# A planner's rank table set anew, and fewer unread products ahead of the first attention score

## The chip, the core and the metric

One core of one Trainium2 chip runs the whole program. The metric is the device time of one launch in microseconds. Five engines work side by side, each through its own list of instructions in order: TensorE (PE in the profile, its weight loads PEld), VectorE (DVE), ScalarE (ACT), GpSimd (POOL) and SyncE (SP), which here issues all DMA transfers.

## The reference

Three layers follow each other on a batch of 4, with 576 tokens and 512 features.

```python
# attention: 8 heads of 64; the first four see a window of 32 keys,
# the other four 32 keys with a dilation of 4
scores = scale * q @ k^T, masked; attn = softmax(scores); x = attn @ v
# first feed-forward layer, with token shift (x_prev is x one token back)
xk = mu_k * x + (1 - mu_k) * x_prev;  xr = mu_r * x + (1 - mu_r) * x_prev
k = relu(xk @ w_k);  v = k * k @ w_v;  r = sigmoid(xr @ w_r);  x = r * v
# second feed-forward layer, with a spatial gate
h = relu(x @ w_in);  u, v = h[..., :512], h[..., 512:]
v = (v - mean(v)) / sqrt(var(v) + 1e-6)
out = (u * (w_spatial @ v + b_spatial)) @ w_out
```

The weights come as 64-bit numbers. The kernel turns them into a high and a low part, and nearly every product of it is a sum of three matmuls (high by high, high by low, low by high).

## The kernel before

The program is written as a list of operations. Each call of `add` records one: what it costs in the planner's estimate on each engine that may do it, the function that emits it, what it reads and writes, and a due time `at`. No operation is emitted when it is recorded. At the end `plan.order()` calls `schedule`, which simulates the engines with these estimates: whenever an engine is free, it takes, of the operations that are ready, the one with the lowest rank. The program is then emitted in the order of the planned starts, and each engine runs its own instructions in that order. So the ranks settle the order on every engine and on SP's list of transfers, and for an operation that two engines may do, which of them does it.

The rank comes from `tuned` and the table `TUNE`. Every operation belongs to a group: a tag such as `('soft', 0, 1)` (softmax, batch 0, second half of the heads) and a kind such as `'mx'`, named after the key it writes. A group has four numbers:

```python
more, grow, dve_, pool_ = TUNE.get(g[0], {}).get(g[1], (0, 0, 792, 22))
prio.append(o[5] + more + grow * (k / count[g]))
self.pens.append({"dve": dve_, "pool": pool_})
```

`o[5]` is the due time, `k` the place of the operation within its group. The last two numbers are handicaps in ns that are added to the end that the planner expects on DVE and on POOL when an operation has a choice of engines.

The due times run from -5000 (first loads) over 1000 for each half of a batch in the first feed-forward layer, 10000 to 11200 for the second layer's first part and 12000 to 13500 for its end. The tags that the prediction uses: `start` and `nat` (first loads, masks, constants), `vw` (values of the attention), `qk` (queries and keys turned), `soft` and `val` (softmax and its product with v), `w` and `w2` (weights loaded and turned into two parts), `k`, `r`, `v` with batch and half (the three products of the first feed-forward layer), `x2`, `u2`, `v2`, `vn`, `ws`, `wsb` (second layer up to the normalised v and the spatial weights), `V`, `vx`, `sp`, `out` (spatial product, gate and last product; the batches come in the order 2, 3, 0, 1).

`order` adds one more thing: where the plan leaves PE idle for more than 60 ns during its first 100 us, it fills the gap with unread products, bf16 matmuls of a constant with itself (224 columns) whose result nobody reads. `end` is the end of PE's last operation; it starts at 500, so the first gap begins there. From `end + 30` on a product is put in every 190 ns in stretches that the plan calls cold, and every 96 ns otherwise, until the next planned operation starts.

In the trace the unread products are the matmuls `psT<-const-bfloat16-1.0`. Nearly every instruction has line L464, since one helper records them all, so the tile names have to be read.

Of the kernel before, what the change touches and what calls it, by code (L numbers as in the profile page):

```python
# [36 lines left out]
def blocks(dil):  # L37
# [38 lines left out]
    ('nat', 0): {'nat': (-2902, -363, 792, 22)},  # L76
    ('nat', 1): {'nat': (5726, -4074, 792, 22)},
    ('out', 0): {'ot': (-3920, 26946, 0, -800), 'out': (-31358, -60293, 1500, -300), 'psB': (135303, 18279, 400, 800)},
    ('out', 1): {'ot': (-60907, 27163, 200, 0), 'out': (52992, 57563, -200, 2000), 'psB': (207273, 5538, 200, -800)},
    ('out', 2): {'ot': (101554, 16247, 200, 22), 'out': (100902, 51712, 200, 800), 'psB': (105659, 29563, 200, -300)},  # L80
    ('out', 3): {'ot': (-109427, -3385, 0, 2000), 'out': (103632, 65781, -600, 800), 'psB': (-41413, -9814, -600, 22)},
# [106 lines left out]
class Plan:  # L188
# [208 lines left out]
    def order(self):  # L397
# [4 lines left out]
        for start, i, e in self.out:  # L402
            if e == "pe":
# [12 lines left out]
                end = self.end[i]  # L416
# [2000 lines left out]
```

## Time and profile before

| what | value |
|---|---|
| three runs, median | 578.58 us |
| three runs, lowest and highest | 575.9 and 580.57 us |
| profiled execution, its own time | 577.68 us |
| span in its profile | 575.9 us |
| mean granted TensorE clock | 0.997 |
| PE busy in the span | 555.1 us |
| DVE, ACT, POOL busy | 435.9, 324.2, 178.2 us |

The span runs from the first to the last instruction of the profiled execution; 1.8 us of its time lie around it. An engine's busy time counts its instructions of arithmetic, the unread products among them, and not the waits.

### The profile page before, as it was taken

How to read it: one execution, taken by the hardware profiler on the slowest of the kernel's cores; microseconds unless marked ns; L12 is line 12 of the kernel's file. 1: busy time of each engine (PE TensorE's matmuls, PEld its weight loads, DVE VectorE, ACT ScalarE, POOL GpSimd, SP SyncE). 2: the span in 40 equal slices, each digit the busy share in tenths (PEclk: the TensorE clock that was granted, in tenths of full speed). 3: DMA queues.
4: the chain of work that ended last, by engine and by line, in shares of the span. 5: the costliest groups of instructions: out<-in, count | busy, mean ns of one | idle time of the engine just before them, and what ended most of it. 6: DMA issues, size and time to landing. Idle time of an engine off the chain costs nothing.

```text
span 575.9 us, 14173 instructions
## 1 busy us (share of the span) xinstructions
PE 555.1 (96%) x5715; PEld 517.2 (90%) x5715; DVE 435.9 (76%) x896; ACT 324.2 (56%) x772; POOL 178.2 (31%) x189
## 2 busy tenths in 40 slices
PE   9788999999999999999999999999989999899996
PEld 8676798789999989999999999999989998689985
DVE  6697999888575898782578955598887789975860
ACT  3578987697372775761657654346553654342331
POOL 1022310544773252210100501036971566422000
PEclk9899999999999999999999999999999999999999
DMA  9879662625944364220023210021010240311012
GB/s 250 224 187 190 180 201 39 103 54 115 130 66 71 101 174 140 66 83 1 1 94 128 74 41 1 26 60 74 1 74 1 60 162 1 110 67 62 1 73 92
DMA packets 95425, 51.55 MB, mean 90 GB/s; under 512 B 77504, under 2 KB 85696, under 8 KB 94848
## 3 DMA queue, kind: packets, MB, share of 16 engines
q1 hardware_dynamic: 95360, 50.65, 33.9%
q8 instruction: 45, 0.74, 0.6%
q14 instruction: 20, 0.16, 0.1%
HBM read 41.72 MB, written 8.91 MB: 88 GB/s over the span
## 4 chain that ended last, share of the span: by engine, by line
PE 67%; DVE 10%; POOL 9%; ACT 7%; issue 6%; DMA 2%; SPq 0%; POOLq 0%; DVEq 0%; ACTq 0%
PE psM L464 42%; PE psB L464 15%; PE psT L464 8%; DVE R L464 2%; PE psS L464 2%; POOL wt L464 2%; ACT L464 1%; POOL sq_dt.float32r L464 1%; DVE wf L464 1%; POOL wsT L464 1%; ACT pt L464 1%; POOL X L464 1%; DMA num<-kept 1%; POOL ws L464 1%; POOL VS L464 1%
## 5 line engine op out<-in xcount | busy, mean ns | idle before, releaser
L464 PE MATMUL psM<-xh,wk 128*128 128x288 f32 x512 | 118.3, 327 | 0.7 <-DVE x L464 0.7
L464 PE MATMUL psM<-sq_dt.float32r,wv 128*128 128x288 f32 x768 | 111.7, 298 | 0.3 <-ACT x L464 0.3
L464 PEld LDWEIGHTS psM<-sq_dt.float32r,wv 128*128 128x128 f32 x768 | 104.1, 189 | 2.0 <-ACT x L464 0.9
L464 PEld LDWEIGHTS psM<-xh,wk 128*128 128x128 f32 x512 | 87.4, 188 | 8.1 <-DVE x L464 0.9
L464 PE MATMUL psM<-xh,wr 128*128 128x288 f32 x256 | 60.2, 302 | 0.4 <-ACT x L464 0.2
L464 POOL TENSOR_TENSOR xl<-xm,xh 128x288 fp32r<-128x288 f32 x25 | 25.5, 1029 | 112.7 <-PE psM L464 35.4
L464 PE MATMUL psM<-xl,wk 128*128 128x288 f32 x192 | 56.4, 294 | 0.0
L464 ACT ACTIVATE kr<-psM 128x288 f32<-128x288 f32 x60 | 24.5, 408 | 39.6 <-PE psM L464 38.0
L464 PE MATMUL psB<-wv,X 128*128 128x256 f32 x336 | 43.7, 284 | 1.8 <-DVE num L464 1.5
L464 PEld LDWEIGHTS psM<-xh,wr 128*128 128x128 f32 x256 | 43.6, 188 | 2.0 <-ACT kr L464 0.7
L464 PEld LDWEIGHTS psB<-wv,X 128*128 128x128 f32 x336 | 41.2, 190 | 2.4 <-issue 1.9
L464 PE MATMUL psM<-X,wu 128*128 128x256 f32 x336 | 42.0, 280 | 0.1
L464 PEld LDWEIGHTS psM<-X,wu 128*128 128x128 f32 x336 | 40.4, 188 | 0.3 <-DVE x L464 0.3
L464 PE MATMUL psB<-wo,gh 128*128 128x512 f32 x128 | 39.6, 391 | 0.0
L464 DVE SCALAR_TENSOR_TENSOR xm<-xd,mu,x 128x288 f32<-128x288 f32 x56 | 35.3, 643 | 4.7 <-POOL xl L464 4.3
L464 PE MATMUL psM<-xl,wr 128*128 128x288 f32 x128 | 37.8, 295 | 0.5 <-POOL xl L464 0.5
L464 POOL TENSOR_TENSOR sq_dt.float32r<-kr,sq_dt.float32r 128x288 fp32r<-128x288 f32 x29 | 25.9, 902 | 35.0 <-ACT sq_dt.float32r L464 19.1
L464 PEld LDWEIGHTS psM<-xl,wk 128*128 128x128 f32 x192 | 36.2, 189 | 0.0
L464 PE MATMUL psT<-const-bfloat16-1.0 128*128 128x224 bf16 x224 | 28.8, 285 | 2.5 <-issue 1.7
L464 ACT ACT_TABLE_LOAD x23 | 29.5, 1283 | 2.8 <-DVE pr L464 1.7
L464 PEld LDWEIGHTS <-const-bfloat16-1.0 128*128 128x128 bf16 x224 | 23.6, 109 | 5.4 <-issue 2.6
L464 ACT CAST xh<-xm 128x288 fp32r<-128x288 f32 x42 | 18.0, 432 | 17.6 <-PE psM L464 8.8
(265 smaller groups left out, 1245.3 us busy)
## 6 DMA issues: line engine op xcount, KB each, us to landing
vw<-in_v_dram SPq DMA_DIRECT2D x36, 128.0 KB, 3.0
room<-in_moe_w_k_dram SPq DMA_DIRECT2D x8, 512.0 KB, 6.0
room<-in_moe_w_v_dram SPq DMA_DIRECT2D x8, 512.0 KB, 3.8
raw<-in_moe_w_in_dram SPq DMA_DIRECT2D x8, 512.0 KB, 3.7
out_dram<-ot SPq DMA_DIRECT2D x16, 256.0 KB, 2.0
ld<-in_k_dram SPq DMA_DIRECT2D x48, 72.0 KB, 2.7
ld<-in_q_dram SPq DMA_DIRECT2D x48, 72.0 KB, 2.5
vw<-in_v_dram SPq DMA_DIRECT2D x16, 144.0 KB, 4.7
```

The costliest lines, as they stand in the source:

```text
L464: return self.tc.keep_in_program_order(getattr(self.engine, name)(*args, **kw))
```

## The change

All 376 groups, in all 128 tags, get new numbers; no group keeps its four. No operation is added, removed or altered, nor any tile, due time or estimate. The second edit is the number from which the first gap of PE is filled. The core of the diff, with the groups of the tags that the prediction speaks of:

```diff
-    ('qk', 0, 0): {'nT': (3175, 2385, 792, 22)},
-    ('nat', 0): {'nat': (-2902, -363, 792, 22)},
-    ('nat', 1): {'nat': (5726, -4074, 792, 22)},
-    ('vw', 0, 0): {'vw': (1947, -223, 792, 22)},
-    ('vw', 0, 1): {'vw': (5562, 774, 792, 22)},
-    ('w', 'wk', 'ld'): {'raw': (226, 4234, 100, 22)},
-    ('r', 0, 0): {'g': (-10371, -5776, 792, 22), 'psM': (9780, -4754, 792, 22), 'xh': (5314, -10237, 1500, 22), 'xl': (-1491, -1640, 792, -800), 'xm': (2724, 1937, 792, 22)},
-    ('v', 0, 1): {'g': (-810, -767, 792, 22), 'psM': (-2066, 2788, 792, 22)},
-    ('vs', 0, 0): {'vw': (11887, 5366, -600, 300)},
-    ('sp', 3): {'R': (19098, -29678, 0, 300), 'egh': (44866, 6324, -600, 800), 'egl': (-152697, -19248, 0, 800), 'gh': (-9562, 27302, 792, 800), 'gl': (-35280, 17202, -200, 800), 'psB': (-34724, -36529, 792, -800), 'psM': (-30995, 34002, 400, 2000)},
...
+    ('qk', 0, 0): {'nT': (61063, -6021, 0, -300)},
+    ('nat', 0): {'nat': (-35649, 3637, -600, 22)},
+    ('nat', 1): {'nat': (5753, -2082, 1500, 2000)},
+    ('vw', 0, 0): {'vw': (-15144, -10511, 0, 2000)},
+    ('vw', 0, 1): {'vw': (5657, 1020, 200, 0)},
+    ('w', 'wk', 'ld'): {'raw': (339, 3820, -200, -300)},
+    ('r', 0, 0): {'g': (-25879, -841, 792, -800), 'psM': (38606, -2525, -600, 0), 'xh': (106286, 3062, 200, -800), 'xl': (18947, -9071, 792, 300), 'xm': (22826, 2592, 0, -300)},
+    ('v', 0, 1): {'g': (12727, 838, 200, 800), 'psM': (78743, 11012, 400, -800)},
+    ('vs', 0, 0): {'vw': (10892, 17667, 1500, 22)},
+    ('sp', 3): {'R': (33493, -87300, -600, 22), 'egh': (121122, -31373, -600, -800), 'egl': (-136220, -3783, 0, 0), 'gh': (67682, 53762, 1500, 300), 'gl': (-29731, 15, -600, -300), 'psB': (-105640, -34734, -200, 2000), 'psM': (-65533, 36135, 1500, 800)},
...
-        res, end, open_, used = [], 500, set(), False
+        res, end, open_, used = [], 5600, set(), False
```

In the table before, many groups of the first batch have the handicaps 792 and 22 that a group without an entry would get, and their ranks are moved by some twenty thousand at most; in the new one most of these handicaps differ, and ranks are moved by up to a hundred thousand.

## Rows read from the trace of the kernel before

**Rows 1.** The page's busy times by engine (us, share of the span, instructions).

```profile
PE 555.1 (96%) x5715; PEld 517.2 (90%) x5715; DVE 435.9 (76%) x896; ACT 324.2 (56%) x772; POOL 178.2 (31%) x189
```

**Rows 2.** Busy time of each engine by stage (stretch, its length, then each engine).

```profile
11.00:84.00 73.00, 65.18 (x1064) 53.15 (x1063) 62.13 (x123) 54.13 (x164) 15.41 (x14) 0.98 0.80 197
60.00:84.00 24.00, 23.39 (x145) 19.90 (x144) 23.65 (x41) 21.58 (x46) 7.65 (x7) 1.00 0.62 167
84.00:400.00 316.00, 314.28 (x3444) 300.65 (x3443) 235.89 (x489) 190.70 (x450) 90.86 (x103) 1.00 0.32 78
400.00:440.00 40.00, 38.20 (x319) 37.65 (x319) 34.12 (x59) 21.12 (x36) 30.32 (x26) 1.00 0.07 27
460.00:505.00 45.00, 40.82 (x274) 37.83 (x274) 42.60 (x85) 20.41 (x43) 26.25 (x26) 1.00 0.26 91
505.00:566.00 61.00, 61.00 (x352) 54.77 (x351) 40.44 (x108) 21.14 (x51) 7.35 (x8) 1.00 0.15 57
```

**Rows 3.** What PE waited for: total us, times, longest.

```profile
PE psM L464 <- DVE wf L464: 3.3, 2, 2.8
PE psT L464 <- issue: 3.0, 2, 1.7
PE psM L464 <- issue: 2.3, 1, 2.3
PE psS L464 <- issue: 1.6, 1, 1.6
PE psB L464 <- DVE num L464: 1.5, 2, 0.8
```

**Rows 4.** The unread products alone, by stretch (PE, PEld, POOL).

```profile
22.70:31.00 8.30, 7.71 (x59) 6.64 (x59) 0.00 (x0) 0.81 0.81 229
31.00:60.00 29.00, 7.21 (x47) 3.77 (x40) 0.00 (x0) 1.00 0.91 194
60.00:84.00 24.00, 3.62 (x28) 2.52 (x28) 0.00 (x0) 1.00 0.62 167
```

**Rows 5.** Timeline of PE, start to first scores (start, us, what, count).

```profile
0.77 10.09 PE L464 MATMUL psT<-const-bfloat16-1.0 128*128 128x224 bf16 x79 [0.77 <-PEq L2400]
...
11.06 0.93 PE L464 MATMUL psM<-turned,turned 32*32 32x64 f32 x48
```

**Rows 6.** PE alone, before and after the step in its pace.

```profile
0.70:5.30 4.60, 4.53 (x25) 1.00 0.74 246
5.40:10.60 5.20, 5.20 (x56) 1.00 1.28 223
```

**Rows 7.** Timeline of DVE and of SP in the first 26 us.

```profile
4.71 4.50 DVE L464 STREAM_TRANSPOSE turned<-early 128x576 f32<-128x576 f32 x4 [2.78 <-DMA early<-in_k_dram]
...
23.07 1.12 DVE L464 COPY pt<-psT 64x384 f32<-64x384 f32 x2 [0.17 <-PE psT L464]
24.12 0.15 DVE L464 TENSOR_SCALAR st<-st 128x6 f32<-128x6 f32 x1
...
14.65 7.91 SPq L464 DMA_DIRECT2D early<-in_v_dram  x6
22.60 2.68 SPq L464 DMA_DIRECT2D room<-in_moe_w_k_dram  x3
```

**Rows 8.** Instructions begun before two stalls of PE end, and the half-clock stretch.

```profile
0.00:16.53 16.53, 13.48 (x223) 11.66 (x223) 11.23 (x14) 7.18 (x21) 1.54 (x9) 1.00 0.98 268
...
0.00:21.63 21.63, 16.96 (x351) 14.21 (x351) 13.50 (x21) 9.49 (x33) 1.54 (x9) 1.00 0.94 238
...
22.50:25.50 3.00, 3.00 (x18) 2.45 (x17) 2.78 (x8) 1.13 (x8) 0.00 (x0) 0.50 0.75 202
```

**Rows 9.** The page's DMA queue of instruction code (packets, MB).

```profile
q8 instruction: 45, 0.74, 0.6%
```

**Rows 10.** The same gate instruction on DVE, in 460:505 and in 505:566 (mean ns).

```profile
L464 DVE SCALAR_TENSOR_TENSOR R<-x,R 128x288 f32<-128x288 f32 x4 | 4.3, 1098 | 0.0
...
L464 DVE SCALAR_TENSOR_TENSOR R<-x,R 128x288 f32<-128x288 f32 x4 | 1.8, 454 | 0.0
```

More of the change, by code (lines that the diff above doesn't have):

```diff
@@ L56 @@
 TUNE = {
[19 rows of a table removed]
-    ('nat', 0): {'nat': (-2902, -363, 792, 22)},
-    ('nat', 1): {'nat': (5726, -4074, 792, 22)},
[L78 to L81, printed above, removed]
[33 rows of a table removed]
@@ L115 @@
-    ('spill', 0): {'spill': (-124049, 2878, 400, 300)},
-    ('spill', 1): {'spill': (-6568, -5613, 0, 0)},
-    ('start',): {'ident': (5243, -7493, 792, 22), 'identb': (-2035, 973, 792, 22), 'mask': (0, 0, 792, 22), 'mask2': (0, 0, 792, 22), 'pt': (7412, 207, 792, 800), 'xok': (11235, 2251, 792, 22)},
-    ('tail',): {'ed': (-37713, -12930, 200, 300), 'eh': (55031, -1110, -200, 800), 'el': (93554, 2871, 200, 300), 'wt': (85684, -68565, 0, 22)},
-    ('tailu', 0): {'psB': (-76264, 25848, 1500, -300), 'utl': (-166368, 9728, 792, 800)},
@@ L120 @@
-    ('tailu', 1): {'psB': (-146359, 49937, 792, 800), 'utl': (-25714, 9413, -200, 22)},
-    ('tailv', 0): {'psB': (-72892, 31446, 1500, 2000), 'vtl': (-76471, -4488, -200, 2000)},
-    ('tailv', 1): {'psB': (-134513, 18615, -200, 0), 'vtl': (-118272, 5243, -600, -300)},
[16 rows of a table removed]
-    ('val', 0, 0): {'psT': (-5281, 5817, 792, 22), 'x': (-16083, -108, 400, 22)},
-    ('val', 0, 1): {'psT': (-3130, -2324, 792, 22), 'x': (4471, 2599, 0, 22)},
-    ('val', 1, 0): {'psT': (3622, 5837, 792, 22), 'x': (-1516, -3804, 0, 22)},
@@ L142 @@
-    ('val', 1, 1): {'psT': (-7539, -7372, 792, 22), 'x': (-9000, 2119, 1500, 22)},
-    ('val', 2, 0): {'psT': (113980, 6146, 400, 0), 'x': (95825, 15957, 1500, 2000)},
-    ('val', 2, 1): {'psT': (-24445, 36013, 792, 300), 'x': (-128732, -34949, -600, -800)},
-    ('val', 3, 0): {'psT': (3444, -13395, 400, 300), 'x': (92914, -58322, 1500, 300)},
-    ('val', 3, 1): {'psT': (-13877, -8819, 792, 0), 'x': (-27787, 36830, 792, 300)},
[16 rows of a table removed]
-    ('w', 'wiu'): {'low': (70028, -40938, -200, 300), 'num': (55346, -605, -600, 800)},
@@ L164 @@
-    ('w', 'wiu', 'ld'): {'raw2': (-52618, -2354, 0, 0)},
-    ('w', 'wiv'): {'low': (130621, -11407, 792, 300), 'num': (215637, -20046, -600, 300)},
[14 rows of a table removed]
-    ('wvroom',): {'wvroom': (0, 0, 792, 22)},
[4 rows of a table removed]
[19 rows of a table added]
+    ('nat', 0): {'nat': (-35649, 3637, -600, 22)},
+    ('nat', 1): {'nat': (5753, -2082, 1500, 2000)},
+    ('out', 0): {'ot': (25583, 2679, 0, 300), 'out': (-144665, -101352, 1500, 0), 'psB': (110898, 7639, 792, -300)},
+    ('out', 1): {'ot': (333, 22848, 1500, 0), 'out': (46189, 64137, 200, 800), 'psB': (225887, 4579, 1500, 0)},
@@ new lines @@
+    ('out', 2): {'ot': (159270, 16910, 1500, -300), 'out': (64073, 69739, 200, 300), 'psB': (26481, 53919, 0, 2000)},
+    ('out', 3): {'ot': (-136582, -8545, 400, 800), 'out': (163805, 39140, 1500, 2000), 'psB': (37793, -6238, 400, 300)},
[33 rows of a table added]
+    ('spill', 0): {'spill': (-110849, 9986, 1500, 2000)},
+    ('spill', 1): {'spill': (-1206, 33896, 400, 2000)},
+    ('start',): {'ident': (46909, -11681, 792, 22), 'identb': (-42650, -12478, -600, 0), 'mask': (7273, -11647, 1500, -800), 'mask2': (-22564, 13200, 400, 800), 'pt': (1497, -6304, 0, -800), 'xok': (19078, -5180, 0, 300)},
@@ new lines @@
+    ('tail',): {'ed': (-26618, 4131, 792, 300), 'eh': (124111, 20405, 200, 2000), 'el': (129364, 56147, 792, 0), 'wt': (183590, -52436, 400, -800)},
+    ('tailu', 0): {'psB': (-75819, 37467, -600, 2000), 'utl': (-134685, 32141, -600, -800)},
+    ('tailu', 1): {'psB': (-231364, 107397, -600, 22), 'utl': (-87552, -749, -200, 0)},
+    ('tailv', 0): {'psB': (-62599, 49372, 200, 800), 'vtl': (-175319, 32396, -200, 800)},
+    ('tailv', 1): {'psB': (-172671, 29059, -200, -300), 'vtl': (-79316, 28163, 400, -800)},
[16 rows of a table added]
@@ new lines @@
+    ('val', 0, 0): {'psT': (76881, 12666, 1500, 300), 'x': (-93718, -12119, 200, 2000)},
+    ('val', 0, 1): {'psT': (24530, 3459, 200, 22), 'x': (21869, 14497, 400, -300)},
+    ('val', 1, 0): {'psT': (3161, 6992, 200, 800), 'x': (22631, -11997, -600, -800)},
+    ('val', 1, 1): {'psT': (-12793, 21083, -200, -800), 'x': (-10891, -7775, 1500, 0)},
+    ('val', 2, 0): {'psT': (163121, 12068, 0, -300), 'x': (122850, 1744, -200, 0)},
+    ('val', 2, 1): {'psT': (-39083, 58929, 400, 800), 'x': (-59515, -45784, -600, -800)},
@@ L185 @@
+    ('val', 3, 0): {'psT': (-57327, -20764, -200, 800), 'x': (101510, -60419, -200, -300)},
+    ('val', 3, 1): {'psT': (19735, -6516, -200, 22), 'x': (16343, 37837, 1500, 800)},
[16 rows of a table added]
+    ('w', 'wiu'): {'low': (-28276, -51119, 792, -800), 'num': (197080, -22641, -600, 300)},
+    ('w', 'wiu', 'ld'): {'raw2': (102589, -31738, 792, 2000)},
+    ('w', 'wiv'): {'low': (113952, 18605, -600, 2000), 'num': (283815, -26707, 200, -800)},
[14 rows of a table added]
+    ('wvroom',): {'wvroom': (-97, -330, 1500, 800)},
[4 rows of a table added]
 }
```

188 rows, old and new, of the table TUNE are left out of this document.

## The prediction

> **What bounds the kernel now.** I began with the page's busy times: PE works for 555.1 us of the 575.9 [rows 1], so no other engine's total is the limit, and the question is what PE does with the other 20.8 us and how much of the 555.1 is work that nobody reads. The table by stage answers the first part. From 84 to 400 us PE is busy for 314.28 of 316.00 us and from 505 to 566 without a break; its idle time lies in 11 to 84 us (7.82), in 400 to 440 (1.80), in 460 to 505 (4.18) [rows 2], and in the two ends. The unread products alone answer the second: 79 of them run before the first score [rows 5], and 59 + 40 + 28 = 127 more between 22.7 and 84 us, counted by their weight loads (the second column) [rows 4]. At full pace one takes 5.20 / 56 = 0.093 us of PE, in the slow pace of the start 4.60 / 25 = 0.18 [rows 6]; 18 of the 127 fall in a stretch with half the clock and take 3.00 / 18 = 0.17 [rows 8]. So they are 127 x 0.093 + 18 x 0.07 = 13.1 us of waiting that looks like work.
>
> So new ranks can earn something in three places only: at the start, in the first batch up to 84 us, and in the second layer from 400 to 505 us. Two of these have another engine at its limit: DVE is busy for 23.65 of 24.00 us from 60 to 84 and for 42.60 of 45.00 from 460 to 505 [rows 2].
>
> **The start.** The second edit can be counted. With `end` at 500 the plan put in 79 products: 16 at a step of 190 until its time 3570, then 63 at 96, until about 9650. If its first score stays there, a start at 5630 leaves (9650 - 5630) / 96, about 42, so 37 fewer. On the chip PE runs 25 of them in its slow pace until 5.3 us, and the other 17 would take 17 x 0.093 = 1.6 us: PE is free at about 7.0. The first score needs the four transposes of q and k, which end on DVE at 4.71 + 4.50 = 9.21 [rows 7]. It now starts at 11.06, behind the 79th product and the mask [rows 5]. It could start at 9.3: 1.7 us earlier, bounded by DVE and no longer by PE.
>
> The ranks must not undo this. By hand: the due time of the first loads is -5000, so the loads of q and k go from -7902 to -40649 and stay first; the mask follows, then the first values. The next ranks are -258 for the second k load, 272 and 832 for the first two w_k loads, 757 upward for the early v loads, much like the old -1281, 159, 771 and 662. SP's list at the start is therefore nearly the same. The transposes get a late rank (-1000 + 61063), behind the copies of v (`vs`, about 8000), but these get a handicap of 1500 on DVE and so go to another engine; DVE has no other ready work then. I take the transposes as unmoved.
>
> How much of the 1.7 us reaches the end? The softmax behind the first scores moves up with them, but six early v loads hold SP's list from 14.65 to 22.56, and three w_k loads wait behind them until 22.60 [rows 7]; their ranks hardly change. What follows is paced by these weights as much as by the scores. I take -1.0.
>
> Code loading speaks here too. PE has started 223 + 223 = 446 instructions when one stall ends and 351 + 351 = 702 when the next does, 256 apart [rows 8]. The waits called "issue" are 3.0 + 2.3 + 1.6 = 6.9 us of PE's idle time [rows 3], about all that PE has from 11 to 84 us (7.82). The code queue moved 45 packets with 0.74 MB [rows 9], 16 KB each. I read these as stops for code where scores use it up fast. With 37 products (74 instructions) fewer, the stop at 702 would meet the instruction that is now at 776, perhaps past the scores, and be hidden: up to 1.6 us more. On the other side, PE's granted clock is half (1.2 of 2.4 GHz) between 22.5 and 25.5 us [rows 8], after two such stops, and cost little because unread products ran there. A new hole from 7 to 9 us could bring such a stretch onto the scores: 3.0 us of them at half clock would cost 1.5. So **start: -1.0, bounds -3.3 and +1.5.**
>
> The Trainium skill (Runtime: NRT & Kernel Launch, section Instruction fetch mechanics) also gives blocks of 256 instructions, and calls the crossing mostly hidden. The trace agrees on the 256 and not on the hiding. If it held here, these 6.9 us would have another cause, open to the ranks, and the sum could be 6.9 us lower.
>
> **The first batch, 11 to 84 us.** The new ranks reorder PE's work: the r product of the first half goes from 1300 + 9780 to 1300 + 38606, the second v product from 2281 - 2066 to 2281 + 78743, behind the k products of batch 0 and much of batch 1. They become work in reserve. Nothing needs their results before the second layer. But a reserve fills a gap only if its inputs are ready, and here they wait for the same DVE. Of the 59 products between 22.7 and 31 [rows 4], those ahead of the third softmax can shrink by the two copies of 1.12 us that stand on DVE ahead of the negation at 24.12 [rows 7], if the order is turned: -1.1. Of the 28 from 60 to 84 I take half, 14 x 0.093 = -1.3. **Taken -2.4.** The lower bound is half of the 13.1 us, -6.6. For the upper bound the nearest rows are those of DVE beside POOL: the same gate instruction takes 1098 ns from 460 to 505, where POOL is busy for 26.25 us, and 454 from 505 to 566, where it is for 7.35 [rows 10, 2]; eight operations of a saturated DVE stretched by 0.64 us give +5.2.
>
> **From 84 to 400 us** DVE is busy for 75% and POOL for 29% [rows 2], so a different order is covered by PE's queue: 0. PE's whole idle time there is 1.7 us, so the bounds are -1.7 and, for a reserve that runs out once, +2. If the cover went, each displaced DVE operation would cost its own 0.4 to 0.7 us.
>
> **From 400 to 505 us** PE waits 3.3 us for `wf` (2.8 of it once) and 1.5 us for `num` [rows 3], on DVE both times. The gate on DVE was drawn out by POOL: three instructions at 0.64 us more are 1.9 us. New ranks set every neighbour of this place differently, so the coincidence is unlikely to return in the same place; with a third of the `num` wait, **-2.4**. Bounds: -6.0 (all idle time of both stretches), and +5 if eight other DVE operations are stretched. What is late next after these is DVE itself, with 2.40 us free in 45. **From 505** on PE is full and the last store is fixed: 0. No wait is added anywhere by name; a new order can only put one behind another.
>
> **Sum.** -1.0 - 2.4 + 0 - 2.4 = -5.8 against the profiled execution's 577.68 us: 571.9. That execution lies 0.9 us under the median of the three runs and inside their spread, so I leave it unshifted: **572 us**, 1.1% under the median. About 1% is what a measurement of this kernel can tell from no change: 572.8 and 584.4 are the borders.
>
> **Rivals.**
> *Pinned.* The w_k loads pace the first batch and DVE the gate, and the new order only moves the waits. For: DVE's 23.65 of 24 us, SP's list. Against: the wait of 2.8 us is one accident of order. Only a part of the start is left: 577.68 - 1.0 = 577.
> *DVE beside POOL (slower).* One mechanism, in the two stretches where DVE is full: each POOL instruction that falls beside a DVE one costs DVE 0.64 us. There are 7 + 26 POOL instructions [rows 2]; 4 DVE ones already carry it [rows 10], so 29 could join. DVE has 0.35 + 2.40 = 2.75 us of cover. With n more the time is 577.68 - 1.0 - 2.75 + 0.64 n, slower by over 1% from n = 17. At 20 it is 586.7. For: handicaps have changed in nearly all groups, in both directions (in the gate of batch 3 DVE's goes from 0 to -600 for `R` and from 792 to 1500 for `gh`). Against: the planner itself slows DVE and POOL beside each other (`until`, rates 0.35 and 0.4), so its order avoids this where its times are right. The Trainium skill (SBUF — State Buffer, section SBUF: two separate sides) says that the two engines' shared ports are an exclusive lock and the loser waits for the whole instruction; the trace agrees in kind, and by that rule the price of a meeting could be a whole POOL instruction, more than 0.64 us.
> *Reserve.* The two products held back fill most gaps of the first batch and all of the gate's waits go: -1.0 - 6.6 - 4 = 566. For: 13.1 us of unread products. Against: DVE.
> *No fewer products in effect*, because the plan's first score moves late: the start gives 0 and the rest stays, 573; it is inside the forecast's range.
>
> **How the numbers follow.** Forecast (568 to 576) 0.40, pinned 0.28, slower 0.18, reserve 0.14. Faster by over 1% is the reserve and three quarters of the forecast: 0.44. Within 1%: a quarter of the forecast and nearly all of pinned, 0.37. Slower: 0.19. The range leaves out 1 in 20 below (561) and about 1 in 8 above (585), past which only the slower rival lies.
>
> **What would show it.** After the change: some 42 unread products ahead of the first score, which starts near 9.3 us, just behind the transposes; fewer than 127 unread products up to 84 us; stalls of PE still 256 instructions apart; no wait of 2.8 us for DVE near 500; PE's idle time from 400 to 505 under 4 us. I am wrong if the first score moves up and the first batch ends no earlier (pinned), if DVE's mean times grow in the two full stretches (slower), or if w_k's loads come earlier than read here.

## The result and the profile after

The changed kernel takes 581.88 us (median of 19 runs, 578.31 to 583.82), the kernel before 578.58 (19 runs beside it, 575.90 to 580.57): a ratio of 1.0056 [1.0038, 1.0073]. That is 3.3 us slower, inside the 1% that was called no change, but on the other side of it than the 572 that I forecast; the interval leaves out 1, so the loss is small and yet clear of the noise. The profiled execution took 581.91 us, with a span of 580.1 and a mean granted clock of 0.988 (0.997 before). Single executions differ in the clock: it is 0.9862 on average over the 19 of the changed kernel, and 0.9906 over the 35 of the kernel before that ran beside `ranks_only`, so the two profiles show more than the usual difference.

First the page's busy times and its row of the granted clock (40 equal slices, in tenths):

```profile
PE 557.5 (96%) x5678; PEld 517.6 (89%) x5678; DVE 431.1 (74%) x866; ACT 314.2 (54%) x749; POOL 223.6 (39%) x242
...
PEclk9888999999999999999999999999999999999999
```

PE has 37 instructions fewer than in [rows 1], all of them unread products, and is busy for 2.4 us more. POOL took over work: 45.4 us more, 242 instructions in place of 189. The clock row has three eights in the first 58 us. The table by stage, to lay beside [rows 2]:

```profile
11.00:84.00 73.00, 64.79 (x978) 52.31 (x968) 58.45 (x126) 53.61 (x162) 10.74 (x10) 0.93 0.78 196
60.00:84.00 24.00, 23.82 (x143) 20.01 (x141) 23.58 (x49) 21.28 (x45) 2.77 (x2) 1.00 0.68 182
84.00:400.00 316.00, 313.23 (x3431) 299.81 (x3431) 236.82 (x473) 179.72 (x429) 119.16 (x135) 1.00 0.31 75
400.00:440.00 40.00, 39.44 (x322) 38.33 (x321) 33.72 (x54) 21.56 (x41) 36.46 (x30) 1.00 0.13 54
...
460.00:505.00 45.00, 40.60 (x284) 38.27 (x284) 42.74 (x84) 20.99 (x45) 27.93 (x27) 1.00 0.31 106
505.00:566.00 61.00, 61.00 (x346) 54.61 (x345) 39.19 (x99) 20.68 (x48) 20.09 (x26) 0.97 0.13 48
```

From 11 to 84 us PE now idles for 8.2 us (7.8 before) and, worse, runs at a mean clock of 0.93 (0.98). From 400 to 440 its idle time fell from 1.80 to 0.56; from 460 to 505 it stayed, 4.40 for 4.18, and the clock dips behind it (0.97 from 505 on). What PE waited for, to lay beside [rows 3]:

```profile
PE psM L464 <- issue: 5.5, 2, 3.2
PE psM L464 <- DVE wf L464: 3.3, 2, 2.9
PE psS L464 <- issue: 2.1, 1, 2.1
```

The wait for `wf` that was to vanish is there with the same 3.3 us. The waits called "issue" have grown from 6.9 us in four pieces to 7.6 in three. Their places are in PE's timeline (start, duration, what, count), which begins as forecast: 42 unread products, and the first scores at 9.32 for 11.06 [rows 5].

```profile
0.78 7.06 PE L464 MATMUL psT<-const-bfloat16-1.0 128*128 128x224 bf16 x42 [0.78 <-PEq L2400]
...
9.32 0.93 PE L464 MATMUL psM<-turned,turned 32*32 32x64 f32 x48
...
16.62 0.51 PE L464 MATMUL psM<-turned,turned 32*32 32x64 f32 x17 [3.25 <-issue]
...
17.70 1.52 PE L464 MATMUL psS<-turned,turned 32*32 32x64 f32 x48
...
32.60 0.39 PE L464 MATMUL psM<-mask,identb 128*128 128x512 bf16 x1
...
33.02 0.88 PE L464 MATMUL psM<-turned,turned 32*32 32x64 f32 x40
36.16 0.42 PE L464 MATMUL psM<-turned,turned 32*32 32x64 f32 x8 [2.25 <-issue]
...
39.69 1.37 PE L464 MATMUL psS<-turned,turned 32*32 32x64 f32 x36
43.17 0.43 PE L464 MATMUL psS<-turned,turned 32*32 32x64 f32 x12 [2.12 <-issue]
...
44.88 2.29 PE L464 MATMUL psM<-xh,wk 128*128 128x288 f32 x4
```

The last two stops cut a group of 48 scores in two, 40 + 8 and 36 + 12. The instructions begun before each of the three stops ends (first and second bracket) are these:

```profile
0.00:16.61 16.61, 11.54 (x223) 8.82 (x223) 9.60 (x11) 8.74 (x22) 3.60 (x11) 1.00 0.99 264
0.00:36.15 36.15, 28.52 (x604) 22.94 (x605) 26.35 (x48) 20.90 (x72) 5.12 (x12) 0.95 0.96 236
0.00:43.16 43.16, 33.43 (x732) 26.39 (x733) 29.50 (x56) 25.34 (x91) 6.77 (x14) 0.92 0.93 227
```

446, 1209 and 1465: 1209 - 446 = 3 x 256 - 5 (a few records of matmuls are missing from a trace), 1465 - 1209 = 256. The stop at 702 [rows 8] is gone, as I thought it might be, but those at 1209 and 1465 stand in the scores for 2.25 and 2.12 us, and the clock falls behind them. In the kernel before, the stops behind 702 stood at 1465 and 1719, for 1.3 and 1.7 us.

### The profile page after: what moved, and what is told of

The parts are those of the page before. It is cut to its first block, busy times and chain, and to the rows that moved or that the text cites. A ratio compares the mean times of both kernels' runs of the same rounds, so it can differ in the third digit from the quotient of the medians.

```text
span 580.1 us, 14149 instructions
## 1 busy us (share of the span) xinstructions
PE 557.5 (96%) x5678; PEld 517.6 (89%) x5678; DVE 431.1 (74%) x866; ACT 314.2 (54%) x749; POOL 223.6 (39%) x242
## 4 chain that ended last, share of the span: by engine, by line
PE 64%; DVE 14%; ACT 8%; POOL 5%; issue 5%; DMA 3%; SPq 0%; DVEq 0%; POOLq 0%; ACTq 0%
PE psM L464 41%; PE psB L464 15%; PE psT L464 6%; DVE R L464 2%; PE psS L464 2%; ACT pr L464 2%; DVE wf L464 1%; ACT L464 1%; DMA ld<-in_q_dram 1%; ACT num L464 1%; DVE st L464 1%; DVE x L464 1%; DVE wt L464 1%; POOL sq_dt.float32r L464 1%; DVE turned L464 1%
## 5 line engine op out<-in xcount | busy, mean ns | idle before, releaser
L464 PE MATMUL psM<-xh,wk 128*128 128x288 f32 x512 | 116.8, 329 | 0.7 <-DVE x L464 0.6
L464 PE MATMUL psM<-sq_dt.float32r,wv 128*128 128x288 f32 x768 | 108.8, 297 | 0.0
L464 PE MATMUL psM<-xh,wr 128*128 128x288 f32 x256 | 58.9, 303 | 0.2 <-ACT kr L464 0.2
L464 POOL TENSOR_TENSOR xl<-xm,xh 128x288 fp32r<-128x288 f32 x31 | 29.8, 969 | 51.1 <-ACT xh L464 38.7
L464 POOL TENSOR_TENSOR sq_dt.float32r<-kr,sq_dt.float32r 128x288 fp32r<-128x288 f32 x34 | 29.9, 889 | 44.6 <-ACT sq_dt.float32r L464 29.6
L464 PE MATMUL psB<-wo,gh 128*128 128x512 f32 x128 | 40.8, 401 | 0.0
L464 ACT ACTIVATE kr<-psM 128x288 f32<-128x288 f32 x54 | 22.0, 408 | 26.3 <-PE psM L464 21.5
L464 POOL TENSOR_TENSOR pr<-pr,st 128x384 f32<-128x384 f32 (+1 forms) x18 | 16.8, 943 | 43.5 <-DVE st L464 42.9
L464 DVE TENSOR_TENSOR x<-psM,x 128x288 f32<-128x288 f32 x32 | 14.2, 451 | 21.5 <-PE psM L464 21.2
```

The lines of the kernel that those rows point to most:

```text
L464: return self.tc.keep_in_program_order(getattr(self.engine, name)(*args, **kw))
```

## The experiments

The times are medians, and the ratios are to the kernel before on the same chip, with their 95% intervals. The kernel before took 577.83 to 578.63 us on these chips, so differences of about 1 us are read from the ratios.

| kernel | us | ratio | interval |
|---|---|---|---|
| changed kernel | 581.88 | 1.0056 | 1.0038 to 1.0073 |
| ranks_only | 577.69 | 0.9977 | 0.9950 to 1.0003 |
| start_only | 580.16 | 1.0008 | 0.9981 to 1.0035 |
| start_66 | 581.49 | 1.0033 | 1.0001 to 1.0065 |
| warm512 | 580.85 | 1.0032 | 1.0003 to 1.0062 |
| wide42 | 583.58 | 1.0073 | 1.0036 to 1.0110 |
| tiny37 | 577.27 | 0.9957 | 0.9929 to 0.9985 |
| tiny64 | 584.70 | 1.0114 | 1.0086 to 1.0142 |
| tiny128 | 584.37 | 1.0105 | 1.0066 to 1.0144 |
| wide21 | 580.34 | 1.0048 | 1.0028 to 1.0069 |
| put_first | 575.29 | 0.9944 | 0.9918 to 0.9970 |
| put_first_42 | 579.99 | 1.0017 | 0.9995 to 1.0039 |
| put_tiny37 | 575.48 | 0.9937 | 0.9914 to 0.9960 |
| whole_v | 580.46 | 1.0043 | 1.0008 to 1.0077 |
| whole_v37 | 576.88 | 0.9991 | 0.9964 to 1.0019 |

**The two halves of the change.** `ranks_only` has the new table and the old start, `start_only` the old table and the new start.

```diff
# ranks_only, against the changed kernel
-        res, end, open_, used = [], 5600, set(), False
+        res, end, open_, used = [], 500, set(), False
# start_only, against the kernel before
-        res, end, open_, used = [], 500, set(), False
+        res, end, open_, used = [], 5600, set(), False
```

> The new table with the old start: 79 unread products ahead of the first score. Theory 'start' (the loss comes from the missing products: PE gets its first scores 1.9 us earlier, meets the same stops for code in other places, and its clock falls to half while scores run): about 578.5 us, within 0.2% of before, granted clock near 0.997, one stretch of half clock ahead of the end. Theory 'ranks' (the loss comes from the new order and the POOL work that grew from 178 to 224 us): about 582 us, as the changed kernel.

> The old table with 42 unread products ahead of the first score. Theory 'start': 581 to 582.5 us, clock 0.98 to 0.99, first score near 9.3 us and the first stop for code still ending near 16.6. Theory 'ranks': 577 to 578.5 us, since the first score is 1.9 us earlier and nothing else changes.

The new ranks alone are level with the kernel before or a little faster (-0.9 us); the new start costs 4.2 us on the new ranks (581.88 - 577.69). On the old ranks a cost is not shown: 580.16 lies 1.5 us over the kernel before and between the ranges of the two theories, and the interval of its ratio takes in 1. So in the changed kernel the start is the loser, not the ranks, and it loses although it does what it says: the scores begin 1.7 us sooner (9.32 for 11.05 in `ranks_only`); on the old ranks two of them begin at 8.01 and the others at 9.09, for 11.06.

**A hole ahead of the scores, or a clock that lacks work?** `start_66` is the kernel before with `end` at 3000 (66 products, first scores near 10.3 us, no hole); `warm512` is the changed kernel with the short products between its score groups 512 columns wide instead of 256.

```diff
# start_66, against the kernel before
-        res, end, open_, used = [], 500, set(), False
+        res, end, open_, used = [], 3000, set(), False
# warm512, against the changed kernel
-    WARM = 256
+    WARM = 512
```

> The old table with 66 unread products (the first gap filled from 3000): they end on the chip near 9.2 us, as the transposes do, so the first score starts near 9.4 and PE has no hole ahead of it. Theory 'start', in the form that the hole and the moved stops for code pull the clock down: between the two, 577 to 580 us, clock nearer to 0.997. In the form that the early scores alone do it: 581 to 582. Theory 'ranks': 577 to 578.5.

> The changed kernel with the 14 unread products inside the first batch's scores twice as wide (512 columns in place of 256): no instruction more, 14 x 0.1 = 1.4 us more PE time at full clock, all in stretches where PE is stopped for code anyway. Theory 'clock' (half clock during the scores is a part of the loss): fewer stretches of half clock up to 50 us than the three of the changed kernel, and 579 to 581 us. If the half clock costs nothing: 582 to 583.5.

Neither is shown to help: 1.0033 without a hole, 1.0032 with more work between the scores. `warm512` lies in the range of its theory 'clock' (580.85), but it is not told apart from the changed kernel, and the mean clock of its trace up to 50 us is the same 0.90. The hole ahead of the mask (0.96 us in the changed kernel) isn't the cause, since `start_66` has none and is no faster than `start_only`, and `wide42`, below, has none on the new ranks. `start_66` lies where I had put it if the early scores alone cost the time (581 to 582), which the next two kernels test. What it shares with the others that lose is that 446 instructions end at another operation than in the kernel before, and a stop at 1209 (35.6 to 37.0 us in its trace, which is of its quickest execution, 578.17 us).

**The place of the stops, or the early start?** Two kernels part them, in opposite directions. `wide42` keeps the changed kernel's count of instructions and gives back the late start; `tiny37` keeps the early start and gives back the count.

```diff
# wide42, against the changed kernel: the first 42 products
...
-nc.tensor.matmul(get(e[0], [P, 512], F32, e[0] + str(e[1]))[:, HALF:], ones[:, :P], ones, start=True, stop=True)
+nc.tensor.matmul(get(e[0], [P, 512], F32, e[0] + str(e[1]))[:, :421], ones[:, :P], long_ones, start=True, stop=True)
# tiny37, against ranks_only: products 43 to 79
...
-nc.tensor.matmul(get(e[0], [P, 512], F32, e[0] + str(e[1]))[:, HALF:], ones[:, :P], ones, start=True, stop=True)
+nc.tensor.matmul(get(e[0], [P, 512], F32, e[0] + str(e[1]))[:32, HALF : HALF + 8], ones[:, :32], ones[:, :8], start=True, stop=True)
```

> The changed kernel with its 42 unread products before the first score 421 columns wide in place of 224, so that they fill TensorE for about as long as the 79 narrow ones of the kernel before: the first score starts near 10.7 us, and the count of TensorE instructions ahead of it stays that of the changed kernel. Theory A, the place of the code fetches: what costs is that the 37 products fewer move the scores' code 74 instructions up, so that stops fall at the instructions numbered 446, 1209 and 1465 (in place of 446, 702, 1465 and 1719), the ones at 1209 and 1465 over 2 us each and with a half clock stretch behind them; this kernel keeps that numbering and takes 581 to 582.5 us. Theory B, the early start: what costs is that the scores begin 1.7 us sooner and run into the first stop with less done ahead of it and TensorE idle for longer; this kernel then has the pace of the ranks alone, 577 to 578.5 us.

> The ranks of the change alone (79 unread products ahead of the first score), with the last 37 of the 79 cut to 32 rows by 8 columns: they keep their 74 instructions but take about 1 us together, so that the first score starts near 9.3 us as in the changed kernel, while the count of instructions ahead of it is that of the kernel before. Theory A, the place of the code fetches: stops at 446, 702, 1465 and 1719 as with the ranks alone, and 576.5 to 577.7 us (up to 1.2 us off the 577.7 of the ranks alone, for the earlier start). Theory B, the early start: the first stop ends where it ends whenever the scores begin, TensorE idles more ahead of it and loses its clock, and the time is 580.5 to 582 us as in the changed kernel.

`wide42` is slow (583.58, 1.1 over its upper guess, with the first scores at 11.48) and `tiny37` fast (577.27): the count of instructions decides, and the early start does no harm. It gives little either, since `tiny37` is not told apart from `ranks_only`: in its trace the first stop lasts 3.54 us for 2.59, and the granted clock is 0.50 from 14.8 to 21.6 us, so on the scores that follow the stop at 15.85. PE's timeline of `tiny37`:

```profile
0.78 7.09 PE L464 MATMUL psT<-const-bfloat16-1.0 128*128 128x224 bf16 x79 [0.78 <-PEq L2404]
...
9.12 0.93 PE L464 MATMUL psM<-turned,turned 32*32 32x64 f32 x48
...
34.49 0.39 PE L464 MATMUL psM<-mask,identb 128*128 128x512 bf16 x1
...
38.66 0.27 PE L464 MATMUL psT<-const-bfloat16-1.0,identb 128*128 128x256 bf16 x1 [0.65 <-issue]
38.86 0.93 PE L464 MATMUL psS<-turned,turned 32*32 32x64 f32 x48
...
40.79 1.24 PE L464 MATMUL psM<-xh,wk 128*128 128x288 f32 x4
```

Two landmarks measure it. The mask of 128x512 ahead of the last scores comes at 32.60 in the changed kernel and at 34.49 here; the first four k products behind them come at 44.88 and 40.79. Over the same work the changed kernel goes from 1.9 us ahead to 4.1 behind: 6.0 us. Its two stops are 2.25 + 2.12 for the one of 0.65, 3.7 us more; most of the other 2.3 is clock, as the windows show (changed kernel, then `tiny37`; the number ahead of the last two is the granted clock, and that behind it the DMA share):

```profile
33.00:37.00 4.00, 1.75 (x69) 1.35 (x70) 3.76 (x10) 2.76 (x14) 0.27 (x1) 1.00 1.22 191
37.00:41.00 4.00, 4.00 (x115) 2.81 (x105) 1.79 (x4) 1.44 (x6) 1.37 (x2) 0.57 0.96 213
```

```profile
33.00:37.00 4.00, 4.00 (x180) 3.02 (x169) 3.73 (x8) 2.41 (x9) 0.00 (x0) 1.00 0.80 200
37.00:41.00 4.00, 3.35 (x133) 2.47 (x133) 3.97 (x10) 3.23 (x13) 2.00 (x2) 1.00 1.02 229
```

From 37 to 41 us the changed kernel's clock is 0.57: 0.43 x 4 = 1.7 us of scores lost, and it falls once more for the k products at 44.88 (2.29 us for the 1.24 of `tiny37`). What follows differs little; at the end the two profiled executions are 581.91 - 577.23 = 4.7 us apart.

`wide42` (first fence) and `tiny128`, below (second), show that the stops are tied to the instructions and not to the time:

```profile
34.99 0.88 PE L464 MATMUL psM<-turned,turned 32*32 32x64 f32 x40
38.16 0.42 PE L464 MATMUL psM<-turned,turned 32*32 32x64 f32 x8 [2.29 <-issue]
...
40.79 0.85 PE L464 MATMUL psS<-turned,turned 32*32 32x64 f32 x36
45.73 0.66 PE L464 MATMUL psS<-turned,turned 32*32 32x64 f32 x12 [4.08 <-issue]
```

```profile
37.88 0.88 PE L464 MATMUL psM<-turned,turned 32*32 32x64 f32 x40
41.19 0.42 PE L464 MATMUL psM<-turned,turned 32*32 32x64 f32 x8 [2.43 <-issue]
...
45.19 0.85 PE L464 MATMUL psS<-turned,turned 32*32 32x64 f32 x36
48.21 0.50 PE L464 MATMUL psS<-turned,turned 32*32 32x64 f32 x12 [2.17 <-issue]
```

The same groups are cut at the same score, 40 + 8 and 36 + 12, though they run 2 and 5 us later than in the changed kernel.

**Other counts ahead of the scores.** `tiny64` and `tiny128` are the changed kernel with so many tiny products ahead of the last of its 42; `wide21` has 21 products of 448 columns in place of the 42.

> The changed kernel with 64 tiny products (128 instructions) behind its 42, half the distance between two stops. Theory, the place of the stops: it is neither the place of the changed kernel nor that of the one with 37 tiny products, so that theory gives only the ends, 577 to 582 us, with stops at the instructions 446, 702 and so on at other operations than in both. Rival, the more instructions ahead the better: at most 577 us.

> The changed kernel with 128 tiny products (32 rows by 8 columns, 256 instructions, about 1 us together) behind its 42: every later instruction moves by 256, which is the distance from one stop to the next, so the stops fall on the same operations as in the changed kernel. Theory, it is the place of the stops among the operations: no gain, stops over 2 us long behind the same scores as the ones at 1209 and 1465 there (now numbered 1465 and 1721), and some 2 to 3 us more ahead of the first stop's fetch, since the first stop then falls 256 instructions earlier in the work and ends where it ends in every kernel: 583 to 585.5 us. Rival, more instructions ahead of the scores help by themselves, whatever their count: 577 us or less, as with 37 tiny ones.

> The changed kernel with 21 unread products of 448 columns in place of its 42 of 224: about the same time of TensorE ahead of the first score (it starts near 9.3 us), but 42 instructions fewer, so that every stop comes 42 instructions later in the work than in the changed kernel. The first stop then begins 0.4 to 0.9 us later and ends where it ends, 0.4 to 0.9 us gained; if the stops behind it are as long as in the changed kernel: 581 to 581.5 us. If that move brings them to a place as good as that of the 37 tiny products: 577 us. Rival, the fewer instructions ahead the worse: 584 us or more.

`tiny128`, shifted by one whole distance between stops, is slow as the theory said (584.37, with the stops in the fences above), and more instructions as such do not help. `tiny64` misses its range: 584.70, over the 582 that I had as its upper end. Its trace, of its quickest execution (581.17 us), has another long stop, this time inside the k products:

```profile
40.23 0.99 PE L464 MATMUL psM<-xh,wk 128*128 128x288 f32 x3
45.00 0.51 PE L464 MATMUL psM<-xh,wk 128*128 128x288 f32 x1 [3.77 <-issue]
```

So the count has good and bad values, and the two kernels that I had taken for the ends of what it can do were not. `wide21` (1.0048) is not told apart from the changed kernel; its stop at 1209 lasts 0.89 us in place of 2.25, the one at 1465 2.47, and its first stop ends at 17.50, not near 16.6 as I had assumed.

The sum of PE's stops goes with the time on the new ranks. Among the kernels with the new ranks and the old gate, the waits called "issue" come to 4.4 (`whole_v37`, below), 5.0 (`tiny37`) and 5.2 us (`ranks_only`) in the three that are no slower than the kernel before, and to 6.5 to 9.6 us in the seven that are, each in its one trace. On the old ranks it does not: 6.9 in the kernel before, 8.9 in `start_only` and 5.1 in `start_66`.

**Why is one stop long and another short?** In the changed kernel the DMA share is high at the first of the two long stops (1.22 from 33 to 37 us, above), but not during the second, where it is 0.33:

```profile
41.00:43.00 2.00, 0.06 (x2) 0.00 (x0) 0.66 (x2) 2.00 (x15) 0.00 (x0) 1.00 0.33 85
```

The next two kernels test whether a code packet that stands behind data makes a stop long. `whole_v` and `whole_v37` bring the plain v loads of the later batches in pieces of 2 KB instead of 256 bytes, on the changed kernel and on `tiny37`.

```diff
...
-vw[KW:, h, :9], vb[h].rearrange("(g p) d -> p g d", p=KW)
+vw[KW:, h, :9], vb[h].rearrange("(p g) d -> p g d", p=KW)
```

> The changed kernel, in which the plain v loads of the later batches (128 and 144 KB each, in pieces of 256 bytes) bring the same number of bytes from consecutive rows, so in pieces of 2 KB (the rows are the wrong ones, so the values that the output is made of are changed); instructions, their order and the bytes stay as they are. Theory, the stops at 1209 and 1465 are long since the packet of code stands behind these loads: the DMA share from 31 to 41 us falls from about 1 to at most 0.7, the two stops (2.25 and 2.12 us) to 1 us or less, and the time to 577.5 to 579.5 us. Rival, the fetch of code takes its time whatever the queues hold: both stops stay at 2 us or more, 581 to 582.5 us.

> The kernel with 37 tiny products behind 42 unread ones, with the same v loads in pieces of 2 KB (wrong rows in the same way). Its stops at 1465 and 1719 are already under 1 us, so by the theory that code waits behind these loads little is left to gain: 576 to 577.5 us. If the loads cost time in another way too (later batches), both kernels gain by the same amount, over 1 us here.

This does not settle it. The share from 31 to 41 us hardly fell in `whole_v` (1.09 to 0.96, row below), so the queues stayed full there, and its stops stayed too: 2.55 and 1.84 us. The time of 580.46 lies between the two guesses and is not told apart from the changed kernel.

```profile
31.00:41.00 10.00, 7.29 (x261) 5.45 (x257) 7.16 (x18) 5.70 (x20) 1.64 (x2) 0.85 0.96 225
```

In `whole_v37` the share fell from 0.81 to 0.64 and the stop of 0.65 us near 38 us is all but gone (PE pauses from 37.64 to 37.75), but by the ratios (0.9991 for 0.9957) it is no faster than `tiny37`. Both fit a packet of code that waits behind data, and neither shows it.

The code queue of the traces settles another part (`--dma` over short windows shows when each 16 KB packet begins). In the sixteen traces, every one of the 53 stops of 0.3 us or more from 9 to 84 us that the waits call "issue" ends 2.4 to 3.5 us after such a packet begins. So these are stops for code, and their length follows from when the packet begins. At 1465 (us):

| kernel | packet begins | PE stops | PE goes on | stop |
|---|---|---|---|---|
| `tiny37` | 36.01 | 38.01 | 38.66 | 0.65 |
| changed kernel | 40.36 | 41.05 | 43.17 | 2.12 |
| `wide42` | 43.14 | 41.65 | 45.73 | 4.08 |

What makes a packet begin when it does stays open. Full queues are not shown to hold it back: ahead of the late one of `wide42` the DMA share is 0.56 from 42 to 43 us.

**The wait at the gate.** PE's wait of 2.88 us near 500 us is for a bank that a sum on DVE frees, and that sum stands behind three gate products. `put_first` (on `ranks_only`), `put_first_42` (on the changed kernel) and `put_tiny37` (on `tiny37`) move this one sum, number 2487 in the list of operations, ahead of the first of the three, number 2541:

```diff
+    steps_ = plan.order()
+    steps_.insert(steps_.index((2541, "dve")), steps_.pop(steps_.index((2487, "dve"))))
-    for i, e in plan.order():
+    for i, e in steps_:
```

> The ranks of the change alone, and one VectorE instruction moved: the sum (wf from x psM, 128x288, 0.44 us) that frees the bank for which TensorE waits 2.88 us near 500 us goes ahead of the three gate products (3.32 us beside GpSimd) behind which it is queued. Theory: the wait costs its whole length and the half clock stretch behind it 1.7 us, since the end of this part is bound by TensorE: 577.7 - 2.9 - 1.7 = 573 us, at least 574.8 if the clock falls elsewhere instead. Rival: the gate products are needed for the outputs just as soon, or TensorE next waits for the bank that the sums behind them free, and the time stays within 0.7 us of 577.7.

> The changed kernel (42 unread products) with the same VectorE sum moved ahead of the three gate products. Theory: the half clock stretch near 505 us and the wait of 2.88 us ahead of it both go: 581.9 - 2.9 - 1.7 = 577.3 us, 579 if only the wait goes; still 3 to 5 us behind the ranks alone with the same move, if the two losses are independent. Rival: within 0.7 us of 581.9.

> The two repairs together: 42 unread products and 37 tiny ones ahead of the first score (the instruction numbers of the kernel before, the early start of the changed one), and the VectorE sum that frees the bank moved ahead of the three gate products. If the two effects are independent: 577.3 (the 37 tiny ones alone) less the 2.4 us that the moved sum gave on the ranks alone, 574.5 to 575.3 us, a ratio to the kernel before of about 0.993. Rival: an earlier start brings another half clock stretch into the first batch, 577 us.

DVE and the two windows of `put_first`:

```profile
495.57 0.44 DVE L464 TENSOR_TENSOR wf<-wf,psM 128x288 f32<-128x288 f32 x1
495.94 4.05 DVE L464 SCALAR_TENSOR_TENSOR R<-x,R 128x288 f32<-128x288 f32 x3
```

```profile
460.00:505.00 45.00, 42.36 (x286) 39.25 (x286) 42.81 (x84) 19.65 (x43) 27.12 (x26) 1.00 0.28 101
505.00:566.00 61.00, 61.00 (x348) 54.47 (x348) 37.38 (x95) 20.61 (x48) 18.77 (x25) 1.00 0.14 53
```

The move gives 2.4 us on the new ranks (577.69 to 575.29), 1.9 on the changed kernel and 1.8 on `tiny37` (0.9957 to 0.9937 by the ratios, so 1.2). Each gain by itself is hardly clear of the noise, but the three agree. That is about half of the 4.6 expected: `put_first` lies between its theory and its rival, `put_first_42` 1 us over its upper guess, `put_tiny37` 0.2. The three gate products are still drawn out by POOL (4.05 us), PE's idle time from 460 to 505 falls to 2.64 us, and the clock stays at 1.00 behind it; but PE then waits for `VS` (0.65 for ACT and 0.45 for DVE near 500 us in `put_tiny37`), the next thing that is late. `put_tiny37` and `put_first` beat the kernel before by 0.6%; they are not told apart from each other.

## Why the prediction was wrong

*The start* (-1.0, bounds -3.3 and +1.5) is the step that failed. Its first half was right: 42 products, first scores at 9.32 for a forecast of 9.3, PE held by the mask and the transposes (4.70 us from 4.57 on). The stop at 702 did get hidden. But I followed the shift of 74 instructions to that one stop and put what it does to the others at nothing. Measured by `ranks_only` the start costs +4.2 us, by `tiny37` its early scores alone give about -0.4 (not told apart from 0): the fewer instructions cost 4.6 (581.88 - 577.27). The half clock I had priced at one stretch of 1.5 us; the trace has it behind each of the three stops and at the gate.

The clock's part can be estimated from the runs too: the mean granted clock is 0.9862 over the 19 runs of the changed kernel and 0.9910 over the 12 of `tiny37`. 0.0048 x 580 = 2.8 of the 4.6 us if PE worked through all of it; among the runs of one kernel 0.001 of clock goes with some 0.4 us (a fit to the runs of all experiments), which would make it 1.9.

My sentence on the Trainium skill (Runtime: NRT & Kernel Launch, section Instruction fetch mechanics), that a crossing of blocks is mostly hidden, would have made the count harmless. The stops that stay open, 7.6 us here and 6.9 before, and the 4.6 us between `tiny37` and the changed kernel, speak against it in this stretch; from 84 to 400 us, where PE is busy for 313.23 of 316.00, it fits.

*The first batch* (-2.4): mis-sized. `ranks_only` idles for 6.3 us from 11 to 84 us against 7.8, and all the ranks together are worth -0.9 with an interval that reaches 0. The products held in reserve did not replace the unread ones: with the start taken out, PE has 5715 instructions as before, so as many unread products, and 145 of them (by their weight loads) run from 11 to 84 us where 127 did. I had forecast fewer.

*84 to 400 us* (0): right within its bounds, 313.23 busy for 314.28.

*400 to 505 us* (-2.4): failed at "the coincidence is unlikely to return in the same place". It returned, 2.9 us for 2.8. The new numbers left the three gate products ahead of the same sum on DVE, and the gate products beside POOL take what they took:

```profile
L464 DVE SCALAR_TENSOR_TENSOR R<-x,R 128x288 f32<-128x288 f32 x4 | 4.3, 1101 | 0.0
```

1101 ns for the 1098 of [rows 10]. That a table is new doesn't mean that an order is. From 400 to 440 the idle time did fall, by 1.2 us, but in the profiled execution the clock behind the wait took as much back (0.03 x 61 = 1.8 us); the one profile of the kernel before, with its high clock, does not show whether it usually loses that too.

*The rivals.* DVE beside POOL did not come: POOL worked 45 us more and the four long gate products stayed four. Pinned (577) comes close to the 577.69 of the ranks alone, but by luck: its only gain was that of the start, which `ranks_only` does not have. The case that came true, a bad count of instructions, I had seen only as a possible gain, at the stop of 702; asked of every stop, it would have been a rival on the slower side. And 1% was too wide for "no change": 19 runs of each kernel were enough to see 0.56%.

## What to carry to other kernels

Where PE stops at fixed distances counted in instructions, adding or taking away instructions ahead moves all the later stops: count how many instructions each edit adds ahead of the dense stretches, and ask of every stop where it lands. Work that nobody reads has two sizes, its time and its instructions, and they can be set apart (tiny products for the count, wide ones for the time). And a new set of ranks is to be judged by the order that it gives: a wait that stands in one place of the list is mended by moving the one operation that it waits for.

## What the hardware showed beside that

- TensorE's stops for code stand 256 of its instructions apart, or a multiple of it, and cut a group of scores at the same one in kernels that reach it up to 5 us later. Their length is not fixed: at 1465 it was 0.65 us (`tiny37`), 2.12 (changed kernel) and 4.08 (`wide42`). They end 2.4 to 3.5 us after their code packet begins, so a packet that begins late makes a long stop; why it begins late stays open.
- The first stop hardly ends sooner when the scores begin sooner: 16.53 us before [rows 8], 16.62 in the changed kernel, which only waits longer there (3.25 us for 2.3 [rows 3]), and 15.85 in `tiny37`. It isn't a fixed time either: it ends at 18.73 in `wide42`, and with the count moved by 256 (`tiny128`) that stop runs from 11.9 to 14.72.
- Behind PE's stops its granted clock fell to half, on scores here: a group of 48 took 0.93 us at 9.32 and 1.52 at 17.70, behind the stop that ends at 16.62, with the granted clock at 0.50 from 17 to 20 us.
